# One VectorE product per unit, deadline order and split ends in a fused spectral mixer and MLP

## The chip, the cores and the metric

The kernel runs on one core of one Trainium2 chip. The metric is the device time of one execution, in microseconds. The profile's "span" is 2 to 3 us shorter than the timed value.

Short names: PE is TensorE, DVE is VectorE, ACT is ScalarE, POOL is GpSimd, SP is SyncE, which only issues DMAs here. PEld in a profile is TensorE's loading of weights. "Evacuated" means copied by ACT or DVE out of PSUM, the memory that matmuls write to, into a tile in SBUF.

## The reference, cut to what matters

```python
x = A_x                                            # [1, 2048, 512] bf16
h  = x + irfft2(rfft2(layernorm(x)) * (w_r + 1j*w_i))   # over tokens and channels
h2 = h + mlp_over_tokens(layernorm(h))             # w1: 2048x1376, gelu, w2: 1376x2048
```

## The kernel before

Both Fourier transforms are made of matmuls with constant matrices. The stages are, in order of data flow:

- f1 (tokens, first half; the layer norm's scale is folded in), to about 20 us;
- f2 (channels), evacuated from PSUM to the tile `CS`;
- x (tokens, second half), whose result stays in PSUM;
- the products with the filter, made by DVE from PSUM into the tile `V`;
- g1 (inverse of x), evacuated to the tile `PQ`;
- g2 and g3 (the inverses of f2 and f1), the residual, the second layer norm;
- the two MLP matmuls, from `HH` and from `GT`.

The change touches f2, x, the products and g1, which are worked through in eight units u = 0 to 7, and the start of g2. g1 has two parities per unit; g2 needs all units of a parity.

A helper records every operation with a modelled duration and a priority. A list scheduler then fixes the order on each engine before the kernel is built: the earliest possible start wins, and at equal starts the priority. On the chip every engine goes through its list in that order, waiting at semaphores. All matmuls therefore have one line number in the profile, and are told apart by tiles: `ps<-EM,Y` is f2, `ps<-CS,EM` is x, `ps<-EM,V` is g1, `ps<-EM,PQ` is g2, `ps<-EO,IF` is g3.

```python
add("Wr", [NP, NG, 257], bf, rw)                     # filter, real part
add("Wi", [NP, NG, 257], bf, rw + 16448)             # imaginary part
add("V", [NP, 2, NG, 256], bf, rv)
# ... (stage_f2: 4 matmuls of 256 columns, priority 10, one evacuation)
def stage_x(u):
    unit = PsumUnit("x", 2)                          # two PSUM banks
    # ... 4 matmuls of 512 columns, priority 13
    for w in range(2):                               # times the real, then the imaginary part
        def tt(s, eng, bank, w=w):
            src = ps[:, bank:bank + 2, :].rearrange("p r (i y j) -> p (r i) y j", i=2, y=2)
            wv = Wx[w][:, 4 * u:4 * u + 4, 1:257].rearrange("p g (j y) -> p g y j", y=2)
            ov = V[:, w, 4 * u:4 * u + 4, :].rearrange("p g (y j) -> p g y j", y=2)
            return eng.tensor_tensor(ov, src, wv, ALU.mult)
        K.op(f"x_{u}_w{w}", "dve", tt, ..., dur=1150.0, unit=unit, pr=True, last=w == 1, prio=11)

def stage_g1(u):
    for par in range(2):
        unit = PsumUnit("g1", 1, early=True)
        # ... 8 matmuls of 128 columns, priority 12: w = 0 for four groups, then w = 1
        evac(f"g1_{u}_{par}_ev", "dve" if u == 7 and par == 1 else "act", dst, src, unit, 512, 12)
```

Of the kernel before, what the change touches and what calls it, by code (L numbers as in the profile page):

```python
# [456 lines left out]
def memory_layout():  # L457
    L = []
    bf = dt.bfloat16
    f32 = dt.float32  # L460
    cur = [0]

    def region(nbytes):
        o = cur[0]
        cur[0] += (nbytes + 31) // 32 * 32
        return o

    def add(name, shape, dty, off):
        L.append((name, shape, dty, off))
        return off  # L470

    ra = region(16384)
    add("X", [NP, NS2, D_LEN], bf, ra)
    for i in range(4):
        for j, nm in enumerate(("U", "Q", "P2", "SG")):
            add(f"{nm}{i}", [NP, D_LEN], bf, ra + (4 * i + j) * 1024)
    rb = region(16384)
    add("PQ", [NP, 2, 2, NS2, NP], bf, rb)
    add("GT", [NP, NFT, D_LEN], bf, rb)
    rc = region(16384)  # L480
    add("Y", [NP, 2, 2, NG, 64], bf, rc)
    add("EO", [NP, NS2, D_LEN], bf, rc)
    add("OUT", [NP, NS2, D_LEN], bf, rc)
    rd = region(16384)
    add("CS", [NP, 16, 2, 256], bf, rd)
    add("H", [NP, NS2, D_LEN], bf, rd)
    rw = region(2 * 16448)
    add("Wr", [NP, NG, 257], bf, rw)
    add("Wi", [NP, NG, 257], bf, rw + 16448)
    add("HH", [NP, NS2, D_LEN], bf, rw)  # L490
    rv = region(32768)
    add("V", [NP, 2, NG, 256], bf, rv)
    r1 = region(NS2 * F_LEN * 2)
    add("W1", [NP, NS2, F_LEN], bf, r1)
    for t in range(NFT):
        add(f"W2_{t}", [NP, S_LEN], bf, rv + t * 4096 if t < 8 else rw + 16448 + (t - 8) * 4096)
    add("FP", [NP, NS2, 2, NP], bf, region(8192))
    add("JK", [NP, 2, D_LEN], bf, region(2048))
    add("FS", [NP, NS2, 2, NP], bf, rv)
    add("EM", [NP, 3328], bf, region(6656))  # L500
    add("IF", [NP, NS2, 2, NP], bf, region(8192))
    for i in (1, 2):
        add(f"st{i}", [NP, NS2, 8], f32, region(512))
        add(f"mv{i}", [NP, NS2, 2], f32, region(128))
        add(f"sd{i}", [NP, NS2], f32, region(64))
        add(f"rs{i}", [NP, NS2], f32, region(64))
        add(f"nb{i}", [NP, NS2], f32, region(64))
        add(f"sx{i}", [NP, NS2], f32, region(64))
        add(f"sq{i}", [NP, NS2], f32, region(64))
    add("eps", [NP, 8], f32, region(32))  # L510
    add("mh", [NP, 8], f32, region(32))
    add("B1s", [NP, 16], bf, region(32))
    add("B1f", [NP, 16], f32, region(64))
    add("B2s", [NP, NS2], bf, region(32))
    add("B2f", [NP, NS2], f32, region(64))
    return L


def build_kernel(nc, A_x, A_w_r, A_w_i, B_w1, B_b1, B_w2, B_b2, out):
# [2 lines left out]
           for k, v in build_consts().items()}  # L522
    es = ExitStack()
    es.__enter__()
    K = Builder(nc, {"f1": 4, "f2": 2, "x": 2, "g1": 2, "g2": 2, "g3": 2, "mm1": 5, "mm1b": 6, "mm2": 8})
    T = K.setup_memory(memory_layout(), es)
    ps = es.enter_context(nc.psum_tensor("ps", [NP, PSUM_BANKS, 512], dt.float32))
    X, FS, Y, CS, V, PQ, EO, H, HH, GT, OUT = (T[n] for n in ("X", "FS", "Y", "CS", "V", "PQ", "EO", "H", "HH", "GT", "OUT"))
    W1, FP, EM, IF, EPS = (T[n] for n in ("W1", "FP", "EM", "IF", "eps"))
    W2 = [T[f"W2_{t}"] for t in range(NFT)]  # L530
    Wx = (T["Wr"], T["Wi"])
    E = EM[:, 0:1024].rearrange("p (b y n) -> p b y n", b=2, y=2)
    M = EM[:, 1024:1792].rearrange("p (i c n) -> p i c n", i=3, c=2)
    R = EM[:, 1792:2304].rearrange("p (i c n) -> p i c n", i=2, c=2)
# [14 lines left out]
            return eng.matmul(outf(bank), lhsT, rhs, start=start, stop=stop, **({"skip_group_check": True} if skip else {}))  # L549
        return K.op(name, "pe", emit, ins=ins or [lhsT, rhs], dur=max(n / 2.4, 55.0), unit=unit, pw=True, first=first, prio=prio)  # L550

    DUR = {"act": {512: 520.0, 1024: 960.0}, "dve": {512: 640.0, 1024: 1150.0}}

    def evac(name, engine, dst, srcf, unit, n, prio, last=True):
        def emit(s, eng, bank):
            if s == "act":
                return eng.activation(dst, srcf(bank), ACT.Copy)  # L557
            return eng.tensor_copy(dst, srcf(bank))  # L558
        return K.op(name, engine, emit, outs=[dst], dur=DUR[engine][n], unit=unit, pr=True, last=last, prio=prio)


    K.op("eps0", "pool", lambda s, eng, bank: eng.memset(EPS[:, 0:1], LN_EPS), outs=[EPS[:, 0:1]], dur=100.0, prio=20)
# [16 lines left out]
    ld_x(12, 16, "act")  # L579
    ld_fp(8, 16)  # L580
    dma("ld_EM", EM[:], cin["EM"][:, :], 6656 * 128, outs=[EM[:]], prio=29)
    def w_cells(w, p0, h0, h1):

        res = [Wx[w][p0:NP:4, h1 - 1:h1, 0:240]]
        if h1 - h0 > 1:
            res.append(Wx[w][p0:NP:4, h0:h1 - 1, :])
        return res

    for g0, g1 in ((0, 8), (8, 16), (16, 32)):
        n = (g1 - g0) * 257  # L590
        h0 = max(g0, 1)
        for w, dram in ((0, A_w_r), (1, A_w_i)):
            for comp in range(2):
                dma(f"ld_w{w}p{comp}_{g0}", Wx[w][comp:NP:4, g0:g1, :], bass.AP(dram.tensor, g0 * 257, [[64 * 257, 32], [1, n]]), 32 * n * 2,
                    outs=w_cells(w, comp, g0, g1), prio=28, rate=330.0)
                p0 = 2 + comp
                if g0 == 0:
                    dma(f"ld_w{w}z{comp}", Wx[w][p0:NP:4, 0:1, :], bass.AP(dram.tensor, 32 * 257, [[64 * 257, 32], [1, 257]]), 32 * 514,
                        outs=w_cells(w, p0, 0, 1), prio=28)
                dma(f"ld_w{w}m{comp}_{g0}", Wx[w][p0:NP:4, h0:g1, :],  # L600
                    bass.AP(dram.tensor, (64 - h0) * 257, [[64 * 257, 32], [-257, g1 - h0], [1, 257]]),
                    32 * (g1 - h0) * 514, outs=w_cells(w, p0, h0, g1), prio=28, rate=330.0)
    B1s, B1f, B2s, B2f = (T[n] for n in ("B1s", "B1f", "B2s", "B2f"))
    dma("ld_IF", IF[:], cin["IF"][:, :, :, :], 1 << 20, outs=[IF[:]], prio=27)
    w1src = B_w1.rearrange("(p s2) f -> p s2 f", s2=NS2)
# [78 lines left out]


    def stage_f2(G):
        unit = PsumUnit("f2", 1)
        for par in range(2):
            for b in range(2):
                mm(f"f2_{G}_{par}{b}", lambda bank, par=par: ps[:, bank, par * 256:par * 256 + 256],  # L690
                   Y[:, b, par, 2 * G:2 * G + 2, :].rearrange("p g k -> p (g k)"), E[:, b, par, :],
                   unit, b == 0, b == 1, par == 0 and b == 0, 10, 256)
        dst = CS[:, G, :, :].rearrange("p c (y j) -> p y c j", y=2)
        evac(f"f2_{G}_ev", "dve" if G in (1, 3) else "act", dst, lambda bank: ps[:, bank, :].rearrange("p (y c j) -> p y c j", y=2, c=2), unit, 512, 10)


    def stage_x(u):
        unit = PsumUnit("x", 2)
        first = True
        for r in range(2):  # L700
            for cs in range(2):
                for i0, n, special in ((0, 1, 2), (1, 1, 0)) if u == 0 and r == 0 else ((0, 2, r),):
                    mm(f"x_{u}_{r}{cs}{i0}", lambda bank, r=r, i0=i0, n=n: ps[:, bank + r, i0 * 256:(i0 + n) * 256],
                       M[:, special, cs, :], CS[:, 2 * u + i0:2 * u + i0 + n, cs, :], unit, cs == 0 and i0 == 0, cs == 1, first, 13, 256 * n,
                       skip=True)
                    first = False
        for w in range(2):
            def tt(s, eng, bank, w=w):
                src = ps[:, bank:bank + 2, :].rearrange("p r (i y j) -> p (r i) y j", i=2, y=2)
                wv = Wx[w][:, 4 * u:4 * u + 4, 1:257].rearrange("p g (j y) -> p g y j", y=2)  # L710
                ov = V[:, w, 4 * u:4 * u + 4, :].rearrange("p g (y j) -> p g y j", y=2)
                return eng.tensor_tensor(ov, src, wv, ALU.mult)  # L712
            K.op(f"x_{u}_w{w}", "dve", tt, ins=[Wx[w][:, 4 * u:4 * u + 4, 1:240]], outs=[V[:, w, 4 * u:4 * u + 4, :]],
                 dur=1150.0, unit=unit, pr=True, last=w == 1, prio=11)


    def stage_g1(u):
        for par in range(2):
            unit = PsumUnit("g1", 1, early=True)
            for w in range(2):  # L720
                for gi in range(4):
                    g = 4 * u + gi
                    mm(f"g1_{g}_{par}{w}", lambda bank, gi=gi: ps[:, bank, gi * NP:gi * NP + NP],
                       V[:, w, g, par * NP:par * NP + NP], R[:, 1 if g == 0 else 0, w, :], unit, w == 0 and gi == 0, w == 1 and gi == 3, gi == 0 and w == 0, 12, 128,
                       skip=True)
            dst = PQ[:, par, :, :, 16 * u:16 * u + 16].rearrange("p q n (g k) -> p (q n) g k", k=4)

            def src(bank):
                return ps[:, bank, :].rearrange("p (g m k) -> p m g k", g=4, k=4)
            evac(f"g1_{u}_{par}_ev", "dve" if u == 7 and par == 1 else "act", dst, src, unit, 512, 12)  # L730

    for u in range(8):
        stage_f2(2 * u)
# [12 lines left out]
           s2 == 0, s2 == NS2 - 1, s2 == 0, 2 if t < 5 else 1, 512)  # L746

    for s2 in range(NS2):
        unit = PsumUnit("g2", 1)
        for par in (1, 0):  # L750
            for pq in range(2):
                mm(f"g2_{s2}_{par}{pq}", lambda bank, par=par: ps[:, bank, (1 - par) * 256:(1 - par) * 256 + 256],
                   PQ[:, par, pq, s2, :], D2[:, par, pq, :], unit, pq == 0, pq == 1, par == 1 and pq == 0, 7, 256)
        evac(f"g2_{s2}_ev", "act", EO[:, s2, :], lambda bank: ps[:, bank, :], unit, 512, 7)
        unit = PsumUnit("g3", 1)
        ev = EO[:, s2, 0:256]
# [115 lines left out]
```

## Time and profile before

| quantity | before |
|---|---|
| time, median | 141.94 us (141.81 to 142.0, 4 runs) |
| span in the profile | 139.9 us |
| PE busy | 122.4 us, at full granted clock |
| first f2 matmul, first product | 20.59, 23.61 us |
| last product ends, first g2 matmul | 44.46, 46.02 us |

The first lines are from the page of the kernel before: busy time of each engine, then its busy share in 40 slices of 3.5 us in tenths, and PE's granted clock.

```profile
PE 122.4 (87%) x754; PEld 76.6 (55%) x754; DVE 81.3 (58%) x169; ACT 64.0 (46%) x138; POOL 18.1 (13%) x49
...
PE   0039779999994899999999999999999999999990
...
DVE  0489966998597399999200779544452324242422
...
PEclk9999999999999999999999999999999999999999
...
```

PE's row is full from the fifteenth slice on. What delays the start of that long stretch delays the end. The row's hole (4 and 8 tenths) is in slices 13 and 14, just before it.

The chain of waits, followed back from the last instruction (start, length, what; all in us), shows the same stretch:

```profile
...
29.40 2.07 ACT PQ L557 x4
31.47 0.05 issue
31.52 5.92 PE ps L549 x62
37.43 0.02 issue
37.45 1.24 DVE V L712
38.69 0.02 issue
38.71 5.76 DVE V L712 x5
44.47 0.05 issue
44.52 0.64 PE ps L549 x8
45.15 0.02 issue
45.18 0.70 DVE PQ L558
45.88 0.14 issue
46.02 2.03 PE ps L549 x16
...
```

From 37.45 to 44.47 us the chain is DVE's products alone, then come eight g1 matmuls, an evacuation of 0.70 us and g2.

The timeline of the same trace (start, length, engine, line, operation, tiles, shapes, count, and in brackets the idle time of the engine before and what ended it):

```profile
...
20.59 1.69 PE L549 MATMUL ps<-EM,Y 128*128 128x256 bf16 x14 [0.97 <-DVE Y L558]
...
33.05 1.28 PE L549 MATMUL ps<-EM,V 128*128 128x128 bf16 x20
...
37.45 1.23 DVE L712 TENSOR_TENSOR V<-ps,Wr 128x1024 bf16<-128x1024 f32 x1 [1.52 <-PE ps L549]
...
43.39 1.75 PE L549 MATMUL ps<-EM,V 128*128 128x128 bf16 x24 [1.50 <-DVE V L712]
...
45.18 0.69 DVE L558 CAST PQ<-ps 128x512 bf16<-128x512 f32 x1 [0.72 <-PE ps L549]
...
46.02 1.58 PE L549 MATMUL ps<-EM,PQ 128*128 128x256 bf16 x13 [0.88 <-DVE PQ L558]
...
```

DVE idles 1.52 us for PE in the middle, and PE idles 1.50 us for DVE at the end: neither is full. The row at 33.05 us is 20 matmuls in 1.28 us.

### The profile page before, as it was taken

How to read it: one execution, taken by the hardware profiler on the slowest of the kernel's cores; microseconds unless marked ns; L12 is line 12 of the kernel's file. 1: busy time of each engine (PE TensorE's matmuls, PEld its weight loads, DVE VectorE, ACT ScalarE, POOL GpSimd, SP SyncE). 2: the span in 40 equal slices, each digit the busy share in tenths (PEclk: the TensorE clock that was granted, in tenths of full speed). 3: DMA queues.
4: the chain of work that ended last, by engine and by line, in shares of the span. 5: the costliest groups of instructions: out<-in, count | busy, mean ns of one | idle time of the engine just before them, and what ended most of it. 6: DMA issues, size and time to landing. Idle time of an engine off the chain costs nothing.

```text
span 139.9 us, 2050 instructions
## 1 busy us (share of the span) xinstructions
PE 122.4 (87%) x754; PEld 76.6 (55%) x754; DVE 81.3 (58%) x169; ACT 64.0 (46%) x138; POOL 18.1 (13%) x49
## 2 busy tenths in 40 slices
PE   0039779999994899999999999999999999999990
PEld 0026557677663666764444444445666666666660
DVE  0489966998597399999200779544452324242422
ACT  3699973767855599984100996533300000000000
POOL 0077700000000003667400000000000000000000
PEclk9999999999999999999999999999999999999999
DMA  4999999999999999500000000000012121212111
GB/s 125 353 391 403 343 356 335 424 415 428 422 288 348 418 274 363 205 0 0 0 5 0 0 0 0 0 0 0 0 42 75 37 75 37 75 42 75 37 49 68
DMA packets 12218, 22.77 MB, mean 163 GB/s; under 512 B 2640, under 2 KB 8784, under 8 KB 11440
## 3 DMA queue, kind: packets, MB, share of 16 engines
q1 hardware_dynamic: 11776, 21.33, 42.5%
q10 hardware_dynamic: 432, 1.31, 2.7%
q8 instruction: 6, 0.10, 0.3%
q14 instruction: 4, 0.03, 0.1%
HBM read 20.54 MB, written 2.10 MB: 162 GB/s over the span
## 4 chain that ended last, share of the span: by engine, by line
PE 75%; DVE 13%; ACT 4%; DMA 3%; POOL 2%; issue 1%; POOLq 0%
PE ps L549 75%; DVE V L712 5%; DMA X<-in_A_x_dram 3%; DVE st_94 L648 2%; POOL FS L657 2%; ACT JK L627 2%; ACT PQ L557 1%; DVE H L763 1%; DVE Y L558 1%; DVE OUT L820 1%; DVE PQ L558 1%; DVE st_101 L769 0%; ACT CS L557 0%; DVE mv_95 L650 0%; DVE FS L657 0%
## 5 line engine op out<-in xcount | busy, mean ns | idle before, releaser
L549 PE MATMUL ps<-HH,W_77 128*128 128x512 bf16 (+1 forms) x176 | 39.8, 379 | 0.2 <-DVE HH L783 0.2
L549 PEld LDWEIGHTS ps<-HH,W_77 128*128 128x128 bf16 (+1 forms) x176 | 17.6, 100 | 19.1 <-issue 0.4
L820 DVE SCALAR_TENSOR_TENSOR OUT<-ps,B2f,H 128x512 bf16<-128x512 f32 x16 | 12.0, 750 | 23.8 <-PE ps L549 23.8
L549 PE MATMUL ps<-FS,X 128*128 128x256 bf16 x64 | 9.4, 315 | 10.2 <-POOL FS L657 10.2
L549 PEld LDWEIGHTS ps<-FS,X 128*128 128x128 bf16 x64 | 6.7, 112 | 12.6 <-POOL FS L657 9.7
L763 DVE TENSOR_TENSOR H<-ps,X 128x512 bf16<-128x512 f32 x16 | 10.4, 675 | 2.2 <-PE ps L549 2.2
L549 PE MATMUL ps<-EM,V 128*128 128x128 bf16 x128 | 9.6, 220 | 1.6 <-DVE V L712 1.5
L557 ACT ACTIVATE PQ<-ps 128x512 bf16<-128x512 f32 x15 | 8.2, 598 | 6.0 <-PE ps L549 5.9
L712 DVE TENSOR_TENSOR V<-ps,Wr 128x1024 bf16<-128x1024 f32 x8 | 9.5, 1220 | 2.3 <-PE ps L549 2.3
L549 PE MATMUL ps<-EM,Y 128*128 128x256 bf16 x64 | 9.1, 273 | 1.3 <-DVE Y L558 1.0
L549 PEld LDWEIGHTS ps<-EM,V 128*128 128x128 bf16 x128 | 7.8, 98 | 3.9 <-DVE V L712 2.3
L549 PE MATMUL ps<-EM,PQ 128*128 128x256 bf16 x64 | 9.1, 272 | 0.9 <-DVE PQ L558 0.9
L712 DVE TENSOR_TENSOR V<-ps,Wi 128x1024 bf16<-128x1024 f32 x8 | 9.5, 1216 | 0.2
L557 ACT ACTIVATE EO<-ps 128x512 bf16<-128x512 f32 x16 | 8.8, 591 | 1.7 <-PE ps L549 1.5
L557 ACT ACTIVATE CS<-ps 128x512 bf16<-128x512 f32 x14 | 7.8, 606 | 3.4 <-PE ps L549 3.4
L627 ACT ACTIVATE JK<-X 128x512 bf16<-128x512 bf16 x14 | 8.6, 613 | 1.2 <-DMA X<-in_A_x_dram 1.2
L549 PE MATMUL ps<-EO,IF 128*128 128x256 bf16 (+1 forms) x48 | 9.1, 308 | 0.0
L627 ACT ACTIVATE JK<-H,nb_98 128x512 bf16<-128x512 bf16 x11 | 7.9, 719 | 2.6 <-DVE H L763 2.4
L648 DVE BATCH_NORM_STATS2 st_94<-X 128x6 f32<-128x512 bf16 x9 | 5.8, 675 | 5.0 <-DMA X<-in_A_x_dram 5.0
L549 PE MATMUL ps<-CS,EM 128*128 128x512 bf16 (+1 forms) x34 | 8.3, 367 | 0.2 <-ACT CS L557 0.2
L549 PEld LDWEIGHTS ps<-EM,Y 128*128 128x128 bf16 x64 | 5.7, 98 | 3.2 <-issue 1.2
L806 DVE TENSOR_TENSOR Q_51<-U_50 128x512 bf16<-128x512 bf16 x3 | 1.3, 423 | 10.5 <-ACT U_50 L804 10.5
(85 smaller groups left out, 194.1 us busy)
## 6 DMA issues: line engine op xcount, KB each, us to landing
W_77<-in_B_w_dram SPq DMA_DIRECT2D x4, 1376.0 KB, 14.4
out_dram<-OUT SPq DMA_DIRECT2D x16, 128.0 KB, 1.8
Wr<-in_A_w_r_dram SPq DMA_DIRECT2D x4, 257.0 KB, 4.3
Wi<-in_A_w_i_dram SPq DMA_DIRECT2D x4, 257.0 KB, 4.6
X<-in_A_x_dram SPq DMA_DIRECT2D x2, 512.0 KB, 7.1
IF<-c_IF SPq DMA_DIRECT2D x1, 1024.0 KB, 6.6
EM<-c_EM SPq DMA_DIRECT2D x1, 832.0 KB, 11.0
Wr<-in_A_w_r_dram SPq DMA_DIRECT2D x6, 128.5 KB, 5.8
```

The lines of the kernel that those rows point to most:

```text
L549: return eng.matmul(outf(bank), lhsT, rhs, start=start, stop=stop, **({"skip_group_check": True} if skip else {}))
L557: return eng.activation(dst, srcf(bank), ACT.Copy)
L558: return eng.tensor_copy(dst, srcf(bank))
L627: K.op(name, "act", lambda s, eng, bank: eng.activation(jk, src, func, accum_out=acc, **kw), ins=[src] + ([bias] if bias is not None else ...
L648: K.op(f"ln1_st{i}", "dve", lambda s, eng, bank, st=st, i=i: eng.bn_stats(st, X[:, i, :]), ins=[X[:, i, :]], outs=[st], dur=600.0, prio=20)
L657: lambda s, eng, bank, i=i, r=r: eng.tensor_scalar(FS[:, i, :, :], FP[:, i, :, :], r, None, op0=ALU.mult),
L712: return eng.tensor_tensor(ov, src, wv, ALU.mult)
L763: K.op(f"h_{s2}", "dve", lambda s, eng, bank, xs=xs, hs=hs: eng.tensor_tensor(hs, ps[:, bank, :], xs, ALU.add), ins=[xs], outs=[hs], dur=6 ...
L806: K.op(f"gelu{t}_q", "dve", lambda s, eng, bank, U=U, Q=Q: eng.tensor_tensor(Q, U, U, ALU.mult), ins=[U], outs=[Q], dur=350.0, prio=5)
L820: K.op(f"fin{s2}", "dve", lambda s, eng, bank, dst=dst, bia=bia, hs=hs: eng.scalar_tensor_tensor(dst, ps[:, bank, :], bia, hs, op0=ALU.add ...
```

## The change

Its intent: the filter's two parts lie side by side, so that one DVE op, which reads the PSUM operand twice through a step of 0, makes both products of a unit. f2 comes before g1 in the priorities, and earlier units before later ones, so that nothing waits for a late product: f2 runs from 12.0 down to 11.25 and g1 from 11.5 to 10.8, so the last units' f2 still stands behind the first units' g1. This is the "deadline order" of the title. The first unit and the last one are cut into smaller pieces. Two evacuations of f2 (G = 1 and 3) and that of unit 7's odd parity move from DVE to ACT.

```diff
-    add("Wr", [NP, NG, 257], bf, rw)
-    add("Wi", [NP, NG, 257], bf, rw + 16448)
+    add("W", [NP, NG, 2, 257], bf, rw)
-    add("V", [NP, 2, NG, 256], bf, rv)
+    add("V", [NP, NG, 2, 256], bf, rv)
 ... (filter loads: chunks of 4, 12 and 16 groups instead of 8, 8 and 16, all in runs of 514 bytes)
 def stage_f2(G):                                  # priority and head
-    ... priority 10; evacuation: "dve" if G in (1, 3) else "act"
+    for pars in ((0,), (1,)) if G == 0 else ((0, 1),):        # first one in two halves, ACT and DVE
+        ... priority 12 - 0.05 * G; evacuation: "dve" if pars[0] else "act"
 def stage_x(u):
+    if u == 0: ... two PSUM units of one bank, four products of 512 elements     # head
-        for w in range(2): ... tensor_tensor over 1024 elements
+        src = bass.AP(src.tensor, src.offset, [list(src.ap[0]), [256, gn], [0, nw], [128, ny], [1, 128]])
+        return eng.tensor_tensor(ov, src, wv, ALU.mult)       # 2048 elements    # merge
+    u == 7: one product of 1024 (odd parity), then two of 512                    # tail
 def stage_g1(u):
-    for par in range(2): ... priority 12
+    for par in (1, 0):   ... priority 11.5 - 0.1 * u
+        split = u == 7 and par == 0     # last evacuation in halves on ACT and DVE   # tail
 ...
-        unit = PsumUnit("g2", 1)
+        unit = PsumUnit("g2", 1, early=s2 < 2)    # odd parity's matmuls may go first  # tail
```

The comments "merge", "head", "tail" and "priority" name the four parts.

More of the change, by code (lines that the diff above doesn't have):

```diff
@@ L524, in build_kernel @@
     es.__enter__()
-    K = Builder(nc, {"f1": 4, "f2": 2, "x": 2, "g1": 2, "g2": 2, "g3": 2, "mm1": 5, "mm1b": 6, "mm2": 8})
+    K = Builder(nc, {"f1": 4, "f2": 2, "x": 2, "g1": 2, "g1t": 2, "g2": 2, "g3": 2, "mm1": 5, "mm1b": 6, "mm2": 8})
     T = K.setup_memory(memory_layout(), es)
@@ L530, in build_kernel @@
     W2 = [T[f"W2_{t}"] for t in range(NFT)]
-    Wx = (T["Wr"], T["Wi"])
+    W = T["W"]
     E = EM[:, 0:1024].rearrange("p (b y n) -> p b y n", b=2, y=2)
@@ L550, in mm, with evac @@
         return K.op(name, "pe", emit, ins=ins or [lhsT, rhs], dur=max(n / 2.4, 55.0), unit=unit, pw=True, first=first, prio=prio)
-    DUR = {"act": {512: 520.0, 1024: 960.0}, "dve": {512: 640.0, 1024: 1150.0}}
-    def evac(name, engine, dst, srcf, unit, n, prio, last=True):
+    DUR = {"act": {256: 310.0, 512: 520.0, 1024: 960.0}, "dve": {256: 350.0, 512: 640.0, 1024: 1150.0}}
+    def evac(name, engine, dst, srcf, unit, n, prio, last=True, outs=None):
         def emit(s, eng, bank):
@@ L558, in emit @@
             return eng.tensor_copy(dst, srcf(bank))
-        return K.op(name, engine, emit, outs=[dst], dur=DUR[engine][n], unit=unit, pr=True, last=last, prio=prio)
+        return K.op(name, engine, emit, outs=outs or [dst], dur=DUR[engine][n], unit=unit, pr=True, last=last, prio=prio)
     K.op("eps0", "pool", lambda s, eng, bank: eng.memset(EPS[:, 0:1], LN_EPS), outs=[EPS[:, 0:1]], dur=100.0, prio=20)
@@ L581, in build_kernel @@
     dma("ld_EM", EM[:], cin["EM"][:, :], 6656 * 128, outs=[EM[:]], prio=29)
-    def w_cells(w, p0, h0, h1):
-        res = [Wx[w][p0:NP:4, h1 - 1:h1, 0:240]]
-        if h1 - h0 > 1:
-            res.append(Wx[w][p0:NP:4, h0:h1 - 1, :])
-        return res
-    for g0, g1 in ((0, 8), (8, 16), (16, 32)):
-        n = (g1 - g0) * 257
+    for g0, g1 in ((0, 4), (4, 16), (16, 32)):
         h0 = max(g0, 1)
@@ L593, in build_kernel @@
             for comp in range(2):
-                dma(f"ld_w{w}p{comp}_{g0}", Wx[w][comp:NP:4, g0:g1, :], bass.AP(dram.tensor, g0 * 257, [[64 * 257, 32], [1, n]]), 32 * n * 2,
-                    outs=w_cells(w, comp, g0, g1), prio=28, rate=330.0)
+                dma(f"ld_w{w}p{comp}_{g0}", W[comp:NP:4, g0:g1, w, :], bass.AP(dram.tensor, g0 * 257, [[64 * 257, 32], [257, g1 - g0], [1, 257]]),
+                    32 * (g1 - g0) * 514, outs=[W[comp:NP:4, g0:g1, w, 0:240]], prio=28, rate=290.0)
                 p0 = 2 + comp
                 if g0 == 0:
-                    dma(f"ld_w{w}z{comp}", Wx[w][p0:NP:4, 0:1, :], bass.AP(dram.tensor, 32 * 257, [[64 * 257, 32], [1, 257]]), 32 * 514,
-                        outs=w_cells(w, p0, 0, 1), prio=28)
-                dma(f"ld_w{w}m{comp}_{g0}", Wx[w][p0:NP:4, h0:g1, :],
+                    dma(f"ld_w{w}z{comp}", W[p0:NP:4, 0:1, w, :], bass.AP(dram.tensor, 32 * 257, [[64 * 257, 32], [257, 1], [1, 257]]), 32 * 514,
+                        outs=[W[p0:NP:4, 0:1, w, 0:240]], prio=28)
+                dma(f"ld_w{w}m{comp}_{g0}", W[p0:NP:4, h0:g1, w, :],
                     bass.AP(dram.tensor, (64 - h0) * 257, [[64 * 257, 32], [-257, g1 - h0], [1, 257]]),
-                    32 * (g1 - h0) * 514, outs=w_cells(w, p0, h0, g1), prio=28, rate=330.0)
+                    32 * (g1 - h0) * 514, outs=[W[p0:NP:4, h0:g1, w, 0:240]], prio=28, rate=290.0)
     B1s, B1f, B2s, B2f = (T[n] for n in ("B1s", "B1f", "B2s", "B2f"))
@@ L686, in stage_f2 @@
     def stage_f2(G):
-        unit = PsumUnit("f2", 1)
-        for par in range(2):
-            for b in range(2):
-                mm(f"f2_{G}_{par}{b}", lambda bank, par=par: ps[:, bank, par * 256:par * 256 + 256],
-                   Y[:, b, par, 2 * G:2 * G + 2, :].rearrange("p g k -> p (g k)"), E[:, b, par, :],
-                   unit, b == 0, b == 1, par == 0 and b == 0, 10, 256)
-        dst = CS[:, G, :, :].rearrange("p c (y j) -> p y c j", y=2)
-        evac(f"f2_{G}_ev", "dve" if G in (1, 3) else "act", dst, lambda bank: ps[:, bank, :].rearrange("p (y c j) -> p y c j", y=2, c=2), unit, 512, 10)
@@ L697, in stage_x @@
-    def stage_x(u):
+        for pars in ((0,), (1,)) if G == 0 else ((0, 1),):
+            unit = PsumUnit("f2", 1)
+            for par in pars:
+                for b in range(2):
+                    mm(f"f2_{G}_{par}{b}", lambda bank, par=par: ps[:, bank, par * 256:par * 256 + 256],
+                       Y[:, b, par, 2 * G:2 * G + 2, :].rearrange("p g k -> p (g k)"), E[:, b, par, :],
+                       unit, b == 0, b == 1, par == pars[0] and b == 0, 12 - 0.05 * G, 256)
+            y = slice(pars[0], pars[-1] + 1)
+            evac(f"f2_{G}_ev{pars[0]}", "dve" if pars[0] else "act", CS[:, G, :, :].rearrange("p c (y j) -> p y c j", y=2)[:, y],
+                 lambda bank, y=y: ps[:, bank, :].rearrange("p (y c j) -> p y c j", y=2, c=2)[:, y], unit, 256 * len(pars), 10)
@@ new lines, in times_filter, with tt @@
+    def times_filter(name, unit, u, srcf, gs, last, ys=slice(0, 2), ws=slice(0, 2)):
+        g0, gn, gk = gs
+        gsl = slice(g0, g0 + (gn - 1) * gk + 1, gk)
+        nw, ny = ws.stop - ws.start, ys.stop - ys.start
+        def tt(s, eng, bank):
+            src = srcf(bank)
+            wv = W[:, gsl, ws, 1:257].rearrange("p g w (j y) -> p g w y j", y=2)[:, :, :, ys, :]
+            ov = V[:, gsl, ws, :].rearrange("p g w (y j) -> p g w y j", y=2)[:, :, :, ys, :]
+            src = bass.AP(src.tensor, src.offset, [list(src.ap[0]), [256, gn], [0, nw], [128, ny], [1, 128]])
+            return eng.tensor_tensor(ov, src, wv, ALU.mult)
+        K.op(name, "dve", tt, ins=[W[:, gsl, ws, 1:240]], outs=[V[:, gsl, ws, ys.start * 128:ys.stop * 128]],
+             dur=gn * nw * ny * 128 / 0.96 + 75.0, unit=unit, pr=True, last=last, prio=11)
@@ new lines, in stage_x @@
+    def stage_x(u):
+        if u == 0:
+            for i in range(2):
+                unit = PsumUnit("x", 1)
+                for r in range(2):
+                    for cs in range(2):
+                        mm(f"x_{u}_{r}{cs}{i}", lambda bank, r=r: ps[:, bank, r * 256:r * 256 + 256],
+                           M[:, 2 if i == 0 and r == 0 else r, cs, :], CS[:, i, cs, :], unit, r == 0 and cs == 0, cs == 1, r == 0 and cs == 0, 13, 256,
+                           skip=True)
+                for w in range(2):
+                    times_filter(f"x_{u}_w{i}{w}", unit, u, lambda bank: ps[:, bank, :], (i, 2, 2), w == 1, ws=slice(w, w + 1))
+            return
@@ L698, in stage_x @@
         unit = PsumUnit("x", 2)
-        first = True
         for r in range(2):
             for cs in range(2):
-                for i0, n, special in ((0, 1, 2), (1, 1, 0)) if u == 0 and r == 0 else ((0, 2, r),):
-                    mm(f"x_{u}_{r}{cs}{i0}", lambda bank, r=r, i0=i0, n=n: ps[:, bank + r, i0 * 256:(i0 + n) * 256],
-                       M[:, special, cs, :], CS[:, 2 * u + i0:2 * u + i0 + n, cs, :], unit, cs == 0 and i0 == 0, cs == 1, first, 13, 256 * n,
-                       skip=True)
-                    first = False
@@ L707, in stage_x @@
-        for w in range(2):
-            def tt(s, eng, bank, w=w):
-                src = ps[:, bank:bank + 2, :].rearrange("p r (i y j) -> p (r i) y j", i=2, y=2)
-                wv = Wx[w][:, 4 * u:4 * u + 4, 1:257].rearrange("p g (j y) -> p g y j", y=2)
-                ov = V[:, w, 4 * u:4 * u + 4, :].rearrange("p g (y j) -> p g y j", y=2)
-                return eng.tensor_tensor(ov, src, wv, ALU.mult)
-            K.op(f"x_{u}_w{w}", "dve", tt, ins=[Wx[w][:, 4 * u:4 * u + 4, 1:240]], outs=[V[:, w, 4 * u:4 * u + 4, :]],
-                 dur=1150.0, unit=unit, pr=True, last=w == 1, prio=11)
@@ L717, in stage_g1 @@
-    def stage_g1(u):
-        for par in range(2):
-            unit = PsumUnit("g1", 1, early=True)
-            for w in range(2):
-                for gi in range(4):
-                    g = 4 * u + gi
-                    mm(f"g1_{g}_{par}{w}", lambda bank, gi=gi: ps[:, bank, gi * NP:gi * NP + NP],
-                       V[:, w, g, par * NP:par * NP + NP], R[:, 1 if g == 0 else 0, w, :], unit, w == 0 and gi == 0, w == 1 and gi == 3, gi == 0 and w == 0, 12, 128,
-                       skip=True)
-            dst = PQ[:, par, :, :, 16 * u:16 * u + 16].rearrange("p q n (g k) -> p (q n) g k", k=4)
-            def src(bank):
-                return ps[:, bank, :].rearrange("p (g m k) -> p m g k", g=4, k=4)
-            evac(f"g1_{u}_{par}_ev", "dve" if u == 7 and par == 1 else "act", dst, src, unit, 512, 12)
+                mm(f"x_{u}_{r}{cs}", lambda bank, r=r: ps[:, bank + r, :], M[:, r, cs, :], CS[:, 2 * u:2 * u + 2, cs, :],
+                   unit, cs == 0, cs == 1, r == 0 and cs == 0, 13, 512)
@@ new lines, in stage_x @@
+        gs = (4 * u, 4, 1)
+        if u < 7:
+            times_filter(f"x_{u}_w", unit, u, lambda bank: ps[:, bank, :], gs, True)
+        else:
+            times_filter(f"x_{u}_w1", unit, u, lambda bank: ps[:, bank, 128:256], gs, False, ys=slice(1, 2))
+            for w in range(2):
+                times_filter(f"x_{u}_w0{w}", unit, u, lambda bank: ps[:, bank, 0:128], gs, w == 1, ys=slice(0, 1), ws=slice(w, w + 1))
+    def stage_g1(u):
+        for par in (1, 0):
+            split = u == 7 and par == 0
+            for gs in ((0, 1), (2, 3)) if split else ((0, 1, 2, 3),):
+                unit = PsumUnit("g1t" if split else "g1", 1, early=True)
+                for w in range(2):
+                    for gi in gs:
+                        g = 4 * u + gi
+                        mm(f"g1_{g}_{par}{w}", lambda bank, gi=gi: ps[:, bank, gi * NP:gi * NP + NP],
+                           V[:, g, w, par * NP:par * NP + NP], R[:, 1 if g == 0 else 0, w, :], unit, w == 0 and gi == gs[0], w == 1 and gi == gs[-1],
+                           w == 0 and gi == gs[0], 11.5 - 0.1 * u, 128, skip=True)
+                ng = len(gs)
+                k0 = 16 * u + 4 * gs[0]
+                dst = PQ[:, par, :, :, k0:k0 + 4 * ng].rearrange("p q n (g k) -> p (q n) g k", k=4)
+                evac(f"g1_{u}_{par}_ev{gs[0]}", "dve" if gs[0] else "act", dst,
+                     lambda bank, gs=gs: ps[:, bank, gs[0] * NP:(gs[-1] + 1) * NP].rearrange("p (g m k) -> p m g k", m=32, k=4), unit, 128 * ng, 12,
+                     outs=[PQ[:, par, gs[0] // 2, :, k0:k0 + 4 * ng]] if split else None)
@@ L752, in build_kernel @@
                 mm(f"g2_{s2}_{par}{pq}", lambda bank, par=par: ps[:, bank, (1 - par) * 256:(1 - par) * 256 + 256],
-                   PQ[:, par, pq, s2, :], D2[:, par, pq, :], unit, pq == 0, pq == 1, par == 1 and pq == 0, 7, 256)
+                   PQ[:, par, pq, s2, :], D2[:, par, pq, :], unit, pq == 0, pq == 1, par == 1 and pq == 0, 7, 256,
+                   ins=[PQ[:, par, :, s2, :], D2[:, par, pq, :]])
         evac(f"g2_{s2}_ev", "act", EO[:, s2, :], lambda bank: ps[:, bank, :], unit, 512, 7)
```

## The prediction

> **What bounds the kernel now.** PE is busy 122.4 of 139.9 us at full granted clock (page part 1, PEclk row), without a break from 52 to 106 us. Whatever moves the start of the last long PE run (51.3 us in the chain of waits) moves the end one to one. The change touches only 20.6 to 46.0 us: f2, x, filter products V, inverse g1. In the chain this stretch is PE and ACT to 37.43, DVE V to 44.47, PE, DVE PQ 0.70, PE 46.02.
>
> From the timeline:
> - DVE makes 16 V products of 1.22 us (groups of line 712): 19.5 us, starting at 23.61 and ending at 44.46. It sits idle about 2.2 us inside, 1.52 at 36 us waiting for PE.
> - PE work there, from runs of back-to-back matmuls: f2 64 x 0.11, x 30 x 0.213 + 4 x 0.11, g1 128 x 0.064, about 22.1 us in 25.4. The idle times named are 1.50 (V), 0.88 (PQ), 0.25 and 0.20 (CS).
> - ACT evacuations take 0.60 us each, some 18 us in all after the change.
>
> **What the change does.**
> 1. One product op of 2048 elements in place of two of 1024. The Trainium skill, "VectorE: DVE Perf Modes", Side-by-side section, gives an op some 158 cycles besides its elements; 1024 + 158 at 0.96 GHz is 1.23 us, which the trace's 1.22 agrees with. The merged op is then an estimated 2.29 us: 0.15 saved, six times. Units 0 and 7 become smaller pieces (4 x 0.68; 1.22 + 2 x 0.68), +0.4 together. DVE sum about 19.1 (was 19.5).
> 2. First unit split: first evacuation halved over ACT and DVE, first product needs one group pair. First V about 22.5 instead of 23.6.
> 3. f2 goes before g1, so products should no longer wait for x; the 1.5 us idle goes. Last V would end near 41.7 (was 44.46).
> 4. Tail: odd parity first, last inverse evacuation halved over ACT and DVE (0.4 instead of 0.7), four g2 matmuls early: 0.3 to 0.7.
> 5. Filter loads all become 514-byte runs: the packet records show 28 ns for 514 B against 164 for 4112 B, so 1.05 MB goes from about 400 to 294 GB/s, 0.95 us more of DMA. They land before use. Off the path.
>
> **What lies on the path.** DVE stops being the limit; PE with 22.1 us of work becomes it. 20.59 + 22.1 + about 0.8 idle at the start (f2 paced by evacuations of 0.60 against 0.44 of matmul) ends g1 near 43.5; the last evacuation adds 0.5, the early g2 work gives back 0.4. So g2 stands as if begun near 43.8 rather than 46.02: 2.2 us gained, passed on in full. Predicted 139.7 us, range 138.6 to 140.9. Chances: faster 0.27, within 2% 0.72, slower 0.01.
>
> **What would show it.** Merged V ops of 2.25 to 2.33 us; first V at 22.3 to 22.8; idle of DVE between V ops under 0.7 in sum; last V near 41.7; first long HH matmul near 49.1 instead of 51.3; PE idle from 20.6 to g2 about 1.3 us instead of 2.8; no V wait for W by DMA.
>
> **What would make it wrong.** If ACT falls behind (it takes over two CS evacuations from DVE), x comes late and DVE idles again. A broadcast PSUM operand could be read more slowly than 1 element a cycle. g1, lowest now, could pile up behind the last V and lengthen the tail.

## The result, and the profile after

The time fell to 138.31 us (median of 4 runs, 138.15 to 138.36) from 141.94. The ratio is 0.9744, with a 95% interval of 0.9727 to 0.9761. The gain of 3.63 us is 1.4 us more than the 2.2 predicted, and the time lies just below the predicted range, which began at 138.6.

The page of the changed kernel:

```profile
PE 120.6 (89%) x747; PEld 77.5 (57%) x756; DVE 79.2 (58%) x165; ACT 64.6 (47%) x141; POOL 18.0 (13%) x49
...
PE   0029779999998999999999999999999999999990
...
DVE  0489985899992899996002686644444242332422
...
PEclk9999999999999999999999999999999999999999
...
```

The hole of 4 and 8 tenths before the long stretch has shrunk to a single 8. (PE's busy time here lacks a few matmul records, so it is not compared.) The chain of waits:

```profile
...
20.56 18.16 PE ps L548 x172
38.73 0.02 issue
38.75 3.54 ACT PQ L556 x7
42.29 0.05 issue
42.34 2.80 PE ps L548 x22
...
```

The chain now stays on PE without a break from the first f2 matmul to 38.73 us, then goes through ACT's evacuations. The timeline:

```profile
...
22.50 2.48 DVE L701 TENSOR_TENSOR V<-ps,W 128x512 bf16<-128x512 f32 x4 [0.88 <-PE ps L548]
...
25.33 15.86 DVE L701 TENSOR_TENSOR V<-ps,W 128x2048 bf16<-128x2048 f32 x9 [0.34 <-PE ps L548]
...
38.21 3.62 PE L548 MATMUL ps<-EM,V 128*128 128x128 bf16 x62
38.75 3.81 ACT L556 ACTIVATE PQ<-ps 128x512 bf16<-128x512 f32 x8 [0.57 <-PE ps L548]
41.88 0.42 DVE L557 CAST PQ<-ps 128x256 bf16<-128x256 f32 x1 [0.69 <-PE ps L548]
42.34 1.70 PE L548 MATMUL ps<-EM,PQ 128*128 128x256 bf16 x14 [0.50 <-ACT PQ L556]
...
```

The first product starts at 22.50 us, as predicted. All other products form one row of 15.86 us without a gap. g1 ends with 62 matmuls in a row at 41.83 us, and g2 starts at 42.34 us, 3.68 us earlier than before.

The groups by form show the merged op (count, then busy us and mean ns of one):

```profile
...
L701 DVE TENSOR_TENSOR V<-ps,W 128x2048 bf16<-128x2048 f32 x6 | 13.3, 2281 | 0.3 <-PE ps L548 0.3
...
```

From the single records of the two traces I worked out how full PE is from the first f2 matmul to the last g1 matmul. Its work is 64 f2 matmuls at 0.109 us from start to start, 32 x matmuls at 0.216 (or as many halves) and 128 g1 matmuls at 0.0558, together 21.03 us; 0.16 us more is the end of the last record. The rest of the stretch is idle:

| | before | change |
|---|---|---|
| first f2 to end of last g1 | 24.55 | 21.28 |
| PE idle in it | 3.35 | 0.08 |
| end of last g1 to first g2 | 0.88 | 0.50 |
| first g2 to end of the last output op | 91.48 | 91.33 |

So the gain is PE's idle time, 3.27 us, and 0.38 us of tail. What came before g2 was passed on to the end in full.

### The profile page after: what moved, and what is told of

Same layout as the page of the kernel before. It is cut to its first block, busy times and chain, and to the rows that moved or that the text cites. A ratio compares the mean times of both kernels' runs of the same rounds, so it can differ in the third digit from the quotient of the medians. Undisturbed runs are those within 1.5% of the kernel's fastest.

```text
span 136.0 us, 2049 instructions
## 1 busy us (share of the span) xinstructions
PE 120.6 (89%) x747; PEld 77.5 (57%) x756; DVE 79.2 (58%) x165; ACT 64.6 (47%) x141; POOL 18.0 (13%) x49
## 2 busy tenths in 40 slices
DMA packets 15929, 22.76 MB, mean 167 GB/s; under 512 B 2640, under 2 KB 12880, under 8 KB 15280
## 4 chain that ended last, share of the span: by engine, by line
PE 80%; ACT 11%; DMA 3%; DVE 3%; issue 1%
PE ps L548 80%; ACT JK L619 6%; DMA X<-in_A_x_dram 3%; ACT PQ L556 3%; ACT sd L611 1%; DVE st L640 1%; DVE Y L557 1%; ACT EO L556 1%; ACT Y L556 1%; DVE OUT L839 1%; DVE mv L642 0%
## 5 line engine op out<-in xcount | busy, mean ns | idle before, releaser
L548 PE MATMUL ps<-HH,W 128*128 128x512 bf16 (+1 forms) x171 | 39.0, 379 | 0.3
L548 PE MATMUL ps<-GT,W 128*128 128x512 bf16 (+1 forms) x172 | 38.0, 379 | 0.2
L548 PEld LDWEIGHTS ps<-GT,W 128*128 128x128 bf16 (+1 forms) x176 | 25.3, 144 | 12.8 <-issue 0.2
L548 PEld LDWEIGHTS ps<-HH,W 128*128 128x128 bf16 (+1 forms) x176 | 17.6, 100 | 18.8
L701 DVE TENSOR_TENSOR V<-ps,W 128x512 bf16<-128x512 f32 (+2 forms) x13 | 18.3, 1463 | 1.3 <-PE ps L548 1.2
L823 ACT ACTIVATE U<-ps,B1f 128x512 bf16<-128x512 f32 (+1 forms) x11 | 7.2, 687 | 14.7 <-PE ps L548 14.7
L556 ACT ACTIVATE CS<-ps 128x512 bf16<-128x512 f32 (+1 forms) x16 | 8.5, 586 | 3.6 <-PE ps L548 3.6
L556 ACT ACTIVATE PQ<-ps 128x512 bf16<-128x512 f32 (+1 forms) x16 | 8.2, 605 | 2.1 <-PE ps L548 2.1
L829 ACT ACTIVATE SG<-P 128x512 bf16<-128x512 bf16 (+1 forms) x11 | 6.6, 624 | 4.7 <-DVE P L828 4.7
L619 ACT ACTIVATE JK<-H,nb 128x512 bf16<-128x512 bf16 x11 | 7.9, 721 | 1.7 <-DVE H L782 1.6
```

The lines of the kernel that those rows point to most:

```text
L548: return eng.matmul(outf(bank), lhsT, rhs, start=start, stop=stop, **({"skip_group_check": True} if skip else {}))
L556: return eng.activation(dst, srcf(bank), ACT.Copy)
L619: K.op(name, "act", lambda s, eng, bank: eng.activation(jk, src, func, accum_out=acc, **kw), ins=[src] + ([bias] if bias is not None else ...
L823: K.op(f"gelu{t}_u", "act", lambda s, eng, bank, U=U, bia=bia, Mt=Mt: eng.activation(U, ps[0:Mt, bank, :], ACT.Identity, bias=bia, scale=1.0),
L829: K.op(f"gelu{t}_sg", "act", lambda s, eng, bank, P2=P2, SG=SG: eng.activation(SG, P2, ACT.Sigmoid, scale=2.0 * GELU_C), ins=[P2], outs=[S ...
```

## The experiments

Theory A, formed from the two traces: the gain is idle time that order and waits had put into PE and DVE, and what an op costs on a full engine is its interval, not its record's length. Its rivals are that the number of ops made it, that the parts simply add up, and that PE alone is the limit now.

For each kernel the table gives the median; the gain against the kernel before in the same rounds (the difference of the medians; the rounds ran on several chips, so gains compare better than medians); PE's idle time and the start of the first g2 matmul, both counted from the first f2 matmul in the profiled run, as above; and the time from first g2 to the end. All runs gave the right result.

| kernel | median us | gain us | ratio | PE idle | first g2 | g2 to end |
|---|---|---|---|---|---|---|
| before | 141.94 | | | 3.35 | 25.43 | 91.48 |
| the change | 138.31 | 3.63 | 0.9744 | 0.08 | 21.78 | 91.33 |
| all_off | 141.97 | 0.12 | 1.0 | 3.29 | 25.36 | 91.48 |
| only_merge | 142.08 | 0.01 | 1.0013 | 2.67 | 24.74 | 91.48 |
| only_prio | 139.96 | 2.13 | 0.9849 | 1.22 | 23.29 | 91.48 |
| only_head | 143.44 | -1.35 | 1.0096 | 4.82 | 26.89 | 91.48 |
| only_tail | 141.22 | 0.92 | 0.9936 | 3.26 | 24.80 | 91.33 |
| no_merge | 139.28 | 2.92 | 0.9797 | 1.25 | 22.29 | 91.93 |
| no_prio | 140.67 | 1.53 | 0.9893 | 2.57 | 23.15 | 92.39 |
| no_head | 138.72 | 3.48 | 0.9758 | 0.34 | 21.72 | 91.60 |
| no_tail | 139.09 | 3.11 | 0.9787 | 0.24 | 22.32 | 91.48 |
| straight | 139.48 | 2.63 | 0.9807 | 1.65 | 22.69 | 91.75 |
| free | 138.64 | 3.50 | 0.9752 | 0.49 | 22.19 | 91.33 |
| x_pe | 141.04 | 1.07 | 0.992 | 0.08 | 24.04 | 91.85 |
| x_dve | 141.58 | 0.53 | 0.9962 | 3.54 | 24.12 | 92.38 |
| tail_dve | 138.87 | 3.24 | 0.9764 | 0.08 | 21.82 | 91.59 |
| best2 | 138.44 | 3.70 | 0.9747 | 0.08 | 21.63 | 91.33 |
| best3 | 138.37 | 3.77 | 0.9735 | 0.08 | 21.64 | 91.33 |
| par7 | 138.89 | 3.15 | 0.9775 | 0.08 | 21.64 | 91.77 |
| par1 | 139.21 | 2.83 | 0.9803 | 0.75 | 21.79 | 91.94 |

In no_merge, no_prio, straight, x_pe, x_dve and par1 the first g2 matmuls go before the last g1 ones, so their g2 starts before g1 is through, and the time from there to the end is longer. There only the sum of the last two columns can be compared.

### Nothing on: all_off

The changed kernel with all four parts undone keeps the new layout and the new loads.

> New layout and new filter loads only; merging, head split, tail split and new priorities all undone, the old order rules. If layout and loads are off the path (theory A): 141.9 us, within 0.2 of before. If the 514-byte loads or the layout cost or gain anything by themselves (rival): a shift of 0.3 us or more, and DVE products that wait for DMA.

It ran as before, ratio 1.0 (0.998 to 1.0019). The layout and the short loads are off the path.

### Each part alone, with the old order otherwise

only_merge, only_prio, only_head and only_tail are all_off with one part switched on again:

```diff
 only_prio:
-  f2 priority 10,               g1 priority 12
+  f2 priority 12 - 0.05 * G,    g1 priority 11.5 - 0.1 * u
 only_merge: one product of 2048 elements in all eight units
 only_head:  f2 G = 0 and x u = 0 in halves, evacuation of G = 1 and 3 on ACT
 only_tail:  u = 7 in three products, last evacuation in halves, odd parity first, early g2
```

> all_off plus one product op of 2048 elements per unit. Theory A (what an op costs back to back is its interval: 2198 ns against 2 x 1131 in the two traces): 8 x 0.064 = 0.5 us less, about 141.4. Rival (what it costs is its duration: 2.28 against 2 x 1.22): 8 x 0.16 = 1.3 us less, about 140.6.

> all_off plus f2 before g1 in the priorities. Theory A (the gain is idle time of PE and DVE that the old order made; DVE idled 2.2 us between its products): 1.5 to 2.3 us less, 139.6 to 140.4. Rival (the old order cost nothing, the number of ops did): under 0.5 us less.

> all_off plus the split first unit. Theory A: first product 1.1 us earlier (22.5 instead of 23.6); passed on in full 140.9 us, if the old order eats it in a later wait of DVE for PE less, 141.3. Rival (start is not on the path): 141.9.

> all_off plus the split last unit, the halved last evacuation and the early g2 matmuls, old priorities. Theory A: the tail is on the path in either order: 0.4 to 0.9 less than before, 141.1 to 141.6. Rival (with the old order it is lost in waits elsewhere, as the split head was): 141.9 or more.

only_prio gained 2.13 us, as theory A said. (Its two halves, f2 ahead of g1 and earlier units ahead of later ones, were not tried apart.) Its DVE row shows why (timeline):

```profile
...
23.75 9.30 DVE L701 TENSOR_TENSOR V<-ps,W 128x1024 bf16<-128x1024 f32 x8 [0.28 <-PE ps L548]
33.23 9.23 DVE L701 TENSOR_TENSOR V<-ps,W 128x1024 bf16<-128x1024 f32 x8 [0.17 <-PE ps L548]
...
```

These are the same 16 products, of the same length, with 0.17 us of idle between two rows of eight. The pause of 1.5 us before has gone, because f2 and x now come in time.

only_merge settles little: its four runs spread from 141.66 to 143.22 us. One of them had a mean granted clock of 0.988 and another took 3.0 us more than its span, where the others took 2.5; in the two plain ones the gain is some 0.4 us. In its profiled run g2 starts 0.62 us earlier than in all_off, which agrees with theory A's 0.5 and not with 1.3.

only_tail gained 0.92 us, at the top of theory A's range.

only_head is a miss: I expected a gain, and it lost 1.35 us. The waits from 20 to 48 us (who waited for whom, total us, times, longest) say how:

```profile
...
DVE V L701 <- PE ps L548: 4.9, 4, 1.7
...
PE ps L548 <- DVE V L701: 3.2, 5, 1.7
...
```

Its first product is 1.1 us earlier, at 22.50 us. But an earlier product lets the scheduler put g1 matmuls, which had the higher priority, in front of f2 and x of later units. PE then stands in front of a g1 matmul whose product is not made (3.2 us), and DVE waits for an x that stands behind it (4.9 us). The two f2 evacuations that only_head moves to ACT are no likely rival: weight loads waited only 0.3 us for ACT's `CS` here, and 1.2 us in all_off. That g1 goes ahead of f2 in the static list is seen in the order of instructions. That this is what makes an early start harmful was not tried by itself, but it fits no_head below, where with the new priorities the same split does no harm.

The gains of the four parts alone add up to 1.7 us (0.01 + 2.13 - 1.35 + 0.92). Together they give 3.63. They do not add.

### Each part taken away from the change

> The change with two product ops of 1024 elements again in the six middle units. Theory A (back to back an op costs its interval): DVE chain of products 6 x 0.064 = 0.4 us longer, and DVE is full from first to last product, so 138.6 to 138.8. Rival (durations count): 6 x 0.15 = 0.9, 139.2.

> The change with the old priorities (g1 before f2). Theory A: most of the gain goes, as DVE waits again between products for PE: 2 to 3.6 us more, 140.3 to 141.9, and with the split head perhaps worse still, as only_head was 1.4 us slower than before. Rival (each part adds its own share): 2.1 more, 140.4.

> The change without the split first unit. Theory A: first product at 23.6 instead of 22.5; DVE's chain has two op starts less, so the last one ends 0.3 to 1.1 us later: 138.6 to 139.4. Rival (the split head costs, as it did alone with the old priorities, where it was 1.4 us slower): below 138.2.

> The change without the split last unit, without the halved last evacuation and without early g2. Theory A: the wait from last g1 matmul to first g2 matmul is 0.88 us again instead of 0.50, and the last unit's products are all late: 0.4 to 0.9 more, 138.7 to 139.2. Rival (the tail is hidden): 138.3.

In gain against before of the same rounds, taking away the priorities costs 2.10 us, merging 0.71, the tail 0.52 and the head 0.15. no_prio (140.67 us) lies within theory A's range, but its loss of 2.10 us is also what the additive rival said (2.13 alone), so this run does not tell the two apart; only_head does. no_tail is as theory A said: the wait from g1 to g2 is 0.87 us again. no_head's median is in theory A's range (138.72 us), but its loss in gain, 0.15 us, is under the 0.3 that it named. no_merge is not as theory A said: by its own median it lost 0.97 us, which is about what the rival, durations, had said (its loss in gain, 0.71, lies between the two), although back to back two ops cost only 0.064 us a unit more than the merged one. That had to be followed up.

### Why two products cost more than one: straight and free

In no_merge the scheduler interleaves: first product of unit 1, first of unit 2, second of unit 1, second of unit 2. Two units' banks are then held longer, and x comes later. My first thought was that this costs the rest. `straight` undoes it with one detail of the model:

```diff
-             dur=..., unit=unit, pr=True, last=last, prio=11)
+             dur=..., unit=unit, pr=True, last=last, prio=11, lat=None if last else 0.0)
```

> no_merge with one scheduling detail changed: the second product of a unit follows the first at once instead of after the first product of the next unit, so a unit's banks come free one product earlier. Still two ops per unit. Theory A2 (of the 0.97 us that no_merge lost, 0.38 is op interval and the rest is banks held longer and DVE then waiting for PE): 138.6 to 138.8, no waits of DVE for PE after the second unit. Rival (the number of ops costs all of it): 139.3 as no_merge.

Its prediction failed: straight was no faster than no_merge (139.48 us). That does not clear the held banks, since the new order brought a wait that no_merge did not have. The records of straight show it. Start to start, the second product of a unit follows the first after 1.25 us, and the first of the next unit follows after 1.14. The second one waits for the semaphore of the first, because the helper makes every reader of a PSUM unit wait for the reader before it. The result does not need that: both only read the banks, and they write different places. `free` takes away what makes it wait:

```diff
-            if rs:
+            if rs and not (pr and "_w" in name):      # products of one unit don't wait for each other
                 deps[id(rs[-1])] = rs[-1]
```

> straight with the same order on every engine, but a product no longer waits for the semaphore of the product before it in the same unit (they only read the bank together and write different places). Theory A3 (straight lost its microsecond because every second product waited for the end of the one before: intervals of 1.25 us instead of 1.13): intervals 1.13, DVE chain about 0.9 us shorter than straight, 138.6 to 138.8. Rival (the number of ops costs it): 139.4 to 139.5 as straight.

The order of instructions of free and straight is the same on all five engines. Their DVE rows (timelines, straight first):

```profile
...
25.70 17.21 DVE L701 TENSOR_TENSOR V<-ps,W 128x1024 bf16<-128x1024 f32 x15 [0.41 <-PE ps L548]
...
```

```profile
...
25.82 15.99 DVE L701 TENSOR_TENSOR V<-ps,W 128x1024 bf16<-128x1024 f32 x15 [0.75 <-PE ps L548]
...
```

The same 15 products take 1.22 us less, and the gain is 0.87 us larger (3.50 against 2.63), at 138.64 us. In free each 1024-element product starts 1131 ns after the one before, though its record is 1210 ns long. So an op that waits for its predecessor's semaphore starts about 0.12 us later than one that does not. The merged op has no such wait inside. So the number of ops is not what costs: two ops in a good order and without the wait are within 0.1 to 0.3 us of the change.

The 0.12 us is what straight lost, not what no_merge lost. In no_merge no product of units 1 to 6 waits for the one just before it:

```profile
...
25.70 16.83 DVE L701 TENSOR_TENSOR V<-ps,W 128x1024 bf16<-128x1024 f32 x15 [0.75 <-PE ps L548]
...
```

From the first product of unit 1 to the first of unit 7 it took 14.15 us, against 13.20 in the change and 13.59 in free. The intervals account for 0.38 of the 0.95 us. Nearly all of the other 0.57 lies in four late starts (1214, 1306, 1261 and 1291 ns after the product before), three of which the trace puts down to a wait for x. That fits my first thought, banks held longer by the interleaving, but no run tried it alone: interleaving without the wait was not built.

Part of the rest between free and the change is unexplained. In no_merge, straight, free and x_dve, the first product of unit 1 starts some 0.4 us later than in the change after the same x matmul. The filter loads that it needs had landed by 21.2 us in all four, so they are not the cause; nothing in the trace says what is.

### Is PE the limit, or DVE: x_pe and x_dve

```diff
 x_pe (g1):
-                for w in range(2):
-                    for gi in gs:
+                for w, gi in [(0, gs[0])] * 3 + [(w, gi) for w in range(2) for gi in gs]:   # 51 more
 x_dve (x, u = 1 to 4; lat = 0 for this op, so that it isn't interleaved):
+                times_filter(f"x_{u}_again", unit, u, ..., (4 * u, 2, 1), False, ws=slice(0, 1))   # 512 elements
```

> The change with 51 g1 matmuls more (the first of each of the 17 g1 groups made four times; the result stays right). If PE is full between first f2 and last g1 and one g1 matmul costs its interval of 0.0558 us: 2.85 us more, 141.1 to 141.2. If one costs the 0.064 of the prediction: 3.3 more, 141.6. If PE has slack there and DVE is the limit: under 1.5 more, below 139.8.

> The change with four products of 512 elements made twice (units 1 to 4; the result stays right), 4 x 0.60 = 2.4 us of DVE work more. If DVE too is full from first to last product (18.34 of 18.69 us): 2.0 to 2.4 more, 140.3 to 140.7. If PE alone limits and DVE has slack, as the prediction said: under 1 more, below 139.3.

The ends of x_pe's stretch (timeline of PE; from its first f2 to the end of 93 matmuls of g1 in a row, and its first g2), and then DVE's row in x_dve, whose 13 products are of several sizes:

```profile
...
20.85 1.36 PE L548 MATMUL ps<-EM,Y 128*128 128x256 bf16 x11 [0.97 <-DVE Y L557]
...
39.62 5.36 PE L548 MATMUL ps<-EM,V 128*128 128x128 bf16 x93
44.89 1.30 PE L548 MATMUL ps<-EM,PQ 128*128 128x256 bf16 x8
...
```

```profile
...
25.69 18.96 DVE L701 TENSOR_TENSOR V<-ps,W 128x512 bf16<-128x512 f32 x13 [0.75 <-PE ps L548]
...
```

With x_pe, the stretch from first f2 to last g1 grew from 21.28 to 24.13 us, which is 2.85 us and so 0.0559 for each of 51 matmuls. PE's idle time stayed at 0.08. The whole lost 2.56 us of gain, as some early g2 work now fills the tail. This settles the disputed cost: 0.056, not 0.064. PE is full.

With x_dve the whole lost 3.10 us, more than either theory said. The added products took 0.71 to 0.83 us from their own start to the next product's, 3.07 in sum and not 4 x 0.60, because the next product of the unit waits for them. With the unexplained 0.4 us that makes the 3.5 us by which DVE's chain from first to last product grew (18.68 to 22.19), of which early g2 work gave some back. Added work lengthens DVE's chain by no less than its own time, and PE then idles 3.54 us. So DVE's chain is full too, and the prediction's sentence that DVE stops being the limit is wrong. In the change the last product ends at 41.19 us and the last g1 matmul at 41.83: both engines arrive together.

### What is left of the tail: tail_dve, best2, best3, par7, par1

In the change ACT evacuates eight g1 units without a pause (the row of 3.81 us above), and g2's first matmul waits 0.50 us behind the last g1. I tried to move one evacuation to DVE, which is idle after its last product.

```diff
 tail_dve: -  "dve" if gs[0] else "act"
           +  "dve" if gs[0] or (u == 7 and par == 1) else "act"
 best3:    +  "dve" if gs[0] or (u, par) == (6, 0) else "act"      (priority of that evacuation 10)
 best2:    best3 and the edit of free
 par7:     best2, g1 priority + 0.25 for the odd parity of units 6 and 7
 par1:     best2, g1 priority + 0.25 for every odd parity
```

> The change with one more evacuation (unit 7, odd parity) on DVE, because in the changed kernel ACT evacuates 8 inverse units without a pause from 38.75 to 42.56 us and the first g2 matmul waits for it 0.5 us behind the last g1 matmul. Theory A (ACT holds the tail): g2 starts 0.3 to 0.5 earlier, 137.8 to 138.0. Rival (the tail is hidden or DVE's evacuation is as late): 138.2 to 138.4.

> The change with the unneeded waits between products of one unit taken out (last products 0.25 us earlier) and one evacuation of unit 6 (even parity) moved from ACT to DVE behind its last product; PE order as in the change. Theory A (ACT's backlog holds the first g2 matmul): g2 starts 0.3 to 0.5 earlier, 137.8 to 138.0. Rival (PE's own work holds all): 138.2 to 138.4.

> The change with only the evacuation of unit 6 moved to DVE. Theory A: 0.2 to 0.5 less, 137.8 to 138.1; the difference to best2 is what the waits between products cost at the end, expected under 0.2 as PE is full there. Rival: 138.2 to 138.4.

> best2 with the odd parity of units 6 and 7 ahead of the even parities in PE's order, so that the early g2 matmuls find their input as soon as g1 ends. Theory A (the order of the last g1 units holds the tail): g2 starts within 0.1 us of the end of g1, 137.9 to 138.1. Rival (then DVE's last evacuation is the wait instead): 138.2 to 138.4.

> best2 with all odd parities a quarter step ahead. Theory A: as par7, 137.9 to 138.1, if the order in the middle does no harm. Rival (any reordering in the middle makes DVE wait for PE somewhere): over 138.4.

tail_dve missed. g2 started no earlier (21.82 against 21.78 us after the first f2), since PE reaches unit 7 only just before its end (DVE's evacuation could not start before 41.58 us and ended at 42.27, where ACT's ended at 42.28 in the change), and the order behind g2 came out worse by 0.26 us. In best2 and best3, PE's order is the change's, and g2 starts 0.14 us earlier. Their times, 138.44 and 138.37 us, with ratios of 0.9747 and 0.9735, can't be told from the change's 0.9744. par7 starts g2 at the same 21.64 us as best3, although the units were reordered, and loses 0.44 us behind it; par1 makes DVE wait 0.88 us for PE in the middle. All five missed theory A's time, and none beats the change clearly. The cause of the last 0.35 us of the tail is not settled further than this: the last g1 unit must be evacuated after PE has made it, and an evacuation of half a unit takes 0.42 us on DVE.

## Why the prediction was wrong

The sum was the right one: PE's work, plus its idle time, plus the tail, passed on in full. Its first two terms were too large.

- **PE's work in the stretch.** This is the term that failed most: "g1 128 x 0.064, about 22.1 us in 25.4". A row of matmuls was divided by its count, and the row includes the end of its last record. From start to start a g1 matmul took 0.0558 us, and x_pe added 51 of them for 2.85 us. The work is 21.03 us, about 1.05 less, nearly all of it g1's (7.14 instead of 8.19). So PE's idle time before was also larger than the prediction's 2.8 us: 3.35 in the stretch and 0.88 behind it. The Trainium skill, "TensorE: Matmul & The Clock Gate", section "Wait — 56ns, not 53.3ns?", gives 55.6 ns from start to start at 128 columns, and this trace agrees.
- **"About 0.8 idle at the start."** It was 0.08 in the whole stretch. f2 and x of the next units and the halves of unit 0 filled it (without the halves, in no_head, it was 0.34). With the work term this puts the end of g1 at 41.83 us instead of "near 43.5", about 1.65 us: the whole miss of 1.4 and some 0.25 more, which the tail takes back.
- **The tail.** The wait behind g1 was 0.50 us, as predicted. The early g2 work was worth 0.15 us (91.48 against 91.33 from first g2 to the end), not 0.4, because the early matmuls had no input before 42.34 us either.
- **The merged op.** Its record is 2.28 us, as estimated. The saving "0.15, six times" came from lengths of records; full intervals give 2 x 1131 - 2198 = 64 ns. Taking the merge away still cost 0.71 to 0.97 us, close to 6 x 0.15, but mostly not through the length of the ops: free, with two ops a unit, is within 0.1 to 0.3 us of the change. The size was right by luck.
- **The last product** ended at 41.19 us instead of 41.7, as from start to start the small products of unit 0 took 0.60 us each and not 0.68, and the merged ones 2.20 and not 2.29; a wait of 0.34 us for x before the first merged one took a part back.
- **"DVE stops being the limit"** is wrong, by x_dve.
- **f2 before g1** was the right reason, and it is the largest part: 2.13 us alone and 2.10 taken away. That a split head alone would do harm was not foreseen.
- **Loads.** They cost more than the 0.95 us predicted: the last filter load landed at 28.47 us instead of 25.91, since 2.1 MB and not 1.05 became short runs (each forward row goes to two partitions). The page's DMA lines show it too: packets under 2 KB rose from 8784 to 12880, and the load of IF, which follows, took 8.5 us to land instead of 6.6. It stayed off the path, as all_off shows.
- **Passed on in full** was right: from the first g2 to the end both kernels take the same within 0.15 us. The marker that I named for it was a bad one: the first HH matmul came at 49.04 us as predicted, only 2.3 us earlier than before while g2 was 3.68 earlier, because the scheduler had put it elsewhere in the list.

## What to carry to other kernels

On a busy engine, cost an op by the interval from its start to the next one's start, taken from single records, never by a row's length over its count: the lengths of records overlap, and here that was worth about 1.05 us of a miss of 1.4. When two engines feed each other through static lists, put the producer of the next unit's input ahead of the consumer of the last one before anything is split: the same split lost 1.35 us under the old order and did no harm under the new. And look for waits that a helper adds without need: a wait for the predecessor's semaphore cost 0.12 us an op, and taking it out of straight, with the order unchanged, brought back 0.87 us of the 1.0 us that straight lay behind the change.

## What the Trainium skill lacked or had wrong

- "VectorE: DVE Perf Modes", section "The DRAIN you can't avoid", says of a chain of copies with a semaphore after each that "the semaphore costs nothing extra here", and that the next op doesn't start before the pipe is empty; it adds, without a number, that an op that is not held starts earlier. In these runs a product that waited for its predecessor's semaphore started about 0.12 us later than one that did not (1247 to 1250 ns against 1131 from start to start at 1024 elements; 725 against 597 at 512), and one without the wait started about 80 ns before the predecessor's record ended. The page's own test is of copies, these are products read from PSUM.
- "TensorE: Matmul & The Clock Gate", section "Back-to-back issue gap", gives about 81 ns per matmul of 128 columns and about 131 per one of 512 for a stream of weight loads and matmuls. Here each g1 matmul has its own weight load, and they follow each other every 55.8 ns; those of 512 columns take 216 ns. The formula for a single one, which that section sets apart, is what this stream obeys.
- "DMA: Bandwidth & Descriptors", section "Specifications", gives 512 B as the smallest transfer for line rate. In the trace of the kernel before, packets of 514 B took a median of 28 ns (18 bytes per ns on one engine) and those of 4112 B took 164 ns (25 bytes per ns), so just above that size a quarter of the rate was still missing. In the change's trace the median of the 514 B packets is 32 ns.
- No page says why a product's start can come about 0.54 us after the end of the matmul that it waits for (free, unit 1), where it was 0.13 us in the change; it is open here too.
